# A new instruction order, engine choice and bank table for a two-layer transformer kernel on one core

## The chip, the core and the metric

The kernel runs on one core of a Trainium2 chip. The core has a matrix engine (TensorE, PE in the profile; its weight loads stand apart as PEld), a vector engine (VectorE, DVE), an engine for activation functions (ScalarE, ACT), a general engine (GpSimd, POOL) and a queue that issues the DMAs (SyncE, SP). Each takes its instructions in order from a queue of its own, and a semaphore makes one wait for another. The metric is device time in microseconds (us), lower is better.

## The reference

The input is one sequence of 2048 rows of 512 bf16 numbers. Four stages, each added to its input:

```python
x = x + A(layernorm(x))   # attention
x = x + B(layernorm(x))   # MLP
x = x + A(layernorm(x))   # the same weights again
x = x + B(layernorm(x))
# A: qkv = x @ wqkv; 32 heads of 16; causal, window of 256 keys;
#    softmax(q k^T / 4) v, then @ wo
# B: gelu(x @ w1 + b1) @ w2 + b2, hidden size 1792
```

## The kernel before, in words

All data stay on chip. The two layers make 32 tiles of 128 rows, handled as 16 *blocks* of two tiles (blocks 0 to 7 are the first layer, 8 to 15 the second). Each step has a name (`key`) that is used below:

- `lnq(b)` (L661): layer norm (`bs`, `ba` statistics on VectorE, `vp` and `pw` the inverse root, `xn` the scaling), a transpose to the layout that the matmul needs (`tx`, a DMA, L632; on TensorE, `tp`, for four tiles at the start and two at the end), and the Q projection (`q{b}_{i}`, steps of two matmuls) with its copy out of the accumulators (`qe`).
- `kv(b)` (L680): the K projection (`k`, copied out with a mask by `ke` on VectorE, L687) and the V projection (`v`, copied out by `ve`). Two DMAs a tile (`vs`, L702) make a second copy of V, moved by 64 rows.
- `attention(b)`: *score groups* `sc{b}_{g}` (L754; ten in a block, five in blocks 0 and 8), each followed by two exponentials on ScalarE (`ex{b}_{g}_0` and `_1`, L761) and one or two masks (`mk`, L782). The *value products* `pv{b}_0` and `pv{b}_1` (L804) take the masked exponentials of the first and the second half of the heads; in a full block one of them is 128 matmuls with their weight loads. Then follow `od` (L813), `rc` (L817), `nm` (L821), `ot` (L827), the output projection `op` and the addition `rs` (L849).
- `mlp(J)`: ten jobs of two or four tiles; the first matrix `m{J}_{fc}`, the bias and gelu on VectorE and ScalarE (`gb` L871, `ga` L874, `ge` L879), the second matrix `y{tau}`, the additions `xb` (L887) and `ya` (L894), and at the end the output DMA.
- `warm0` to `warm17` (L539): matmuls on zeros, put into the PE queue. Seven of them are 32 columns wide (`WSHORT`), the others 512.

These steps are 3098 nodes of a plan. What runs where and when is not computed but read from three tables: `_ORDER` is one list of all node numbers (each engine's queue is its own nodes in that order), `_ALT` lists the nodes that run on their second engine (a mask or `nm` on GpSimd in place of VectorE; `ve`, `qe` or `te` on ScalarE in place of VectorE; `vp` on VectorE in place of GpSimd), and `_BANKS` gives, in the order of use, the first of the eight accumulator banks that each group of matmuls takes. `_Plan.run` (L393) reads them, and asserts that no node stands before one that it depends on and that a bank is free:

```python
for i in _ALT:
    nodes[i]["eng"], nodes[i]["fn"] = nodes[i]["alts"][1]
for i in _ORDER:
    for g, k in nd["alloc"]:
        b = next(banks)
        gmap[g] = tuple(range(b, b + k))
```

`_Sched.op` (L62) then adds the waits: a step waits for whoever wrote what it reads, and for whoever last used what it overwrites, a bank among others. So a score group cannot start before an earlier exponential, copy or addition has emptied the banks that the table gives it.

Of the kernel before, what the change touches and what calls it, by code (L numbers as in the profile page):

```python
# [19 lines left out]
class _Sched:  # L20
# [147 lines left out]
    15, 34, 5, 0, 6, 14, 35, 7, 33, 28, 38, 29, 47, 8, 18, 23, 9, 36, 3, 26, 31, 10, 57, 37, 11, 22, 1, 40, 4, 24,  # L168
    2, 58, 59, 61, 17, 42, 62, 21, 60, 65, 41, 63, 19, 64, 68, 55, 32, 66, 107, 39, 69, 67, 20, 105, 50, 70, 3097,
    48, 30, 27, 53, 25, 106, 108, 71, 109, 49, 72, 110, 73, 16, 74, 114, 81, 75, 82, 111, 83, 84, 115, 85, 86, 116,  # L170
    112, 87, 88, 89, 113, 195, 153, 117, 127, 128, 151, 196, 129, 130, 154, 118, 152, 131, 119, 197, 155, 120, 156,
    98, 99, 100, 121, 12, 101, 90, 13, 102, 367, 91, 368, 104, 159, 92, 93, 157, 94, 103, 325, 76, 369, 199, 77,
    326, 95, 78, 200, 79, 370, 132, 80, 133, 96, 134, 135, 201, 323, 97, 203, 198, 137, 136, 158, 138, 205, 144,
    139, 202, 140, 145, 204, 141, 146, 160, 147, 122, 520, 217, 148, 123, 206, 124, 219, 143, 125, 208, 126, 46,
    218, 324, 43, 213, 209, 327, 328, 215, 166, 167, 168, 331, 169, 214, 207, 371, 176, 329, 177, 521, 373, 210,
    178, 330, 216, 179, 522, 171, 172, 180, 372, 161, 173, 211, 142, 174, 170, 56, 375, 220, 162, 376, 332, 163,
    164, 523, 175, 524, 221, 374, 377, 150, 212, 165, 149, 380, 378, 222, 188, 382, 189, 44, 190, 181, 45, 525,
    182, 381, 223, 385, 183, 224, 191, 386, 184, 384, 226, 225, 227, 54, 231, 232, 387, 379, 233, 526, 234, 383,
    333, 228, 185, 343, 388, 389, 334, 192, 229, 235, 344, 395, 194, 230, 335, 396, 345, 238, 346, 291, 390, 236,
    397, 239, 237, 347, 240, 336, 241, 348, 337, 349, 338, 242, 350, 244, 339, 243, 391, 399, 351, 401, 340, 341,  # L180
    352, 400, 245, 403, 342, 392, 402, 51, 353, 405, 52, 354, 355, 398, 356, 186, 360, 404, 357, 361, 362, 527,
    363, 393, 408, 364, 253, 409, 260, 261, 407, 254, 262, 410, 359, 413, 255, 246, 247, 415, 411, 256, 412, 257,
    248, 249, 250, 258, 414, 406, 564, 251, 273, 394, 274, 566, 263, 276, 416, 267, 268, 417, 565, 264, 270, 271,
    265, 277, 642, 285, 286, 423, 567, 418, 640, 275, 643, 528, 287, 529, 428, 272, 419, 282, 252, 283, 429, 288,
    259, 289, 641, 420, 308, 290, 309, 421, 424, 266, 310, 311, 279, 278, 644, 269, 422, 645, 284, 307, 280, 312,
    281, 313, 314, 315, 540, 425, 426, 568, 427, 541, 570, 316, 648, 542, 543, 649, 317, 569, 544, 318, 530, 531,
    319, 532, 187, 533, 572, 534, 193, 320, 574, 321, 646, 430, 431, 322, 647, 292, 573, 293, 294, 432, 577, 295,
    435, 579, 366, 576, 296, 545, 297, 436, 358, 571, 298, 433, 578, 546, 582, 434, 547, 437, 584, 548, 575, 550,
    438, 899, 551, 552, 650, 583, 553, 439, 651, 441, 652, 440, 653, 554, 900, 897, 585, 592, 654, 299, 549, 300,
    301, 593, 365, 302, 303, 304, 442, 581, 305, 594, 586, 535, 536, 898, 580, 596, 537, 306, 598, 538, 587, 901,  # L190
    539, 902, 597, 595, 600, 588, 557, 601, 660, 661, 662, 663, 599, 602, 605, 664, 558, 559, 607, 560, 655, 656,
    561, 457, 458, 606, 603, 610, 903, 657, 589, 658, 612, 904, 604, 453, 590, 459, 454, 476, 455, 477, 611, 485,
    486, 563, 609, 479, 591, 480, 482, 562, 613, 659, 470, 471, 483, 556, 905, 464, 465, 467, 478, 468, 484, 608,
    450, 460, 469, 461, 906, 451, 466, 446, 452, 447, 481, 443, 487, 448, 444, 473, 472, 462, 665, 474, 456, 614,
    666, 667, 445, 463, 615, 449, 475, 616, 684, 625, 626, 668, 617, 489, 686, 620, 618, 490, 491, 492, 685, 493,
    619, 621, 494, 669, 688, 687, 627, 690, 628, 622, 629, 495, 488, 623, 689, 496, 632, 692, 497, 694, 498, 624,
    691, 499, 500, 501, 630, 502, 693, 697, 504, 631, 505, 633, 1017, 506, 698, 507, 508, 634, 509, 1018, 510, 503,
    635, 699, 511, 702, 1019, 670, 512, 704, 700, 671, 672, 1020, 695, 673, 1021, 703, 674, 712, 696, 513, 514,
    701, 676, 714, 515, 706, 516, 517, 705, 518, 713, 519, 716, 638, 707, 717, 715, 718, 833, 720, 708, 721, 677,
    917, 1022, 918, 919, 709, 722, 920, 719, 710, 725, 921, 678, 727, 679, 680, 724, 681, 726, 730, 922, 636, 923,  # L200
    1023, 731, 912, 924, 728, 1024, 913, 723, 914, 915, 732, 729, 925, 711, 941, 637, 943, 734, 907, 908, 909, 733,
    910, 916, 926, 555, 735, 942, 639, 1025, 911, 736, 945, 934, 946, 935, 675, 737, 947, 738, 683, 949, 1026, 936,
    739, 948, 951, 937, 740, 938, 741, 742, 682, 950, 743, 944, 954, 744, 745, 955, 746, 747, 750, 952, 748, 940,
# [762 lines left out]
```

## Time and profile before

| what | value |
|---|---|
| time, median of 3 runs | 442.14 us (442.01 to 442.3) |
| profiled execution: span | 442.4 us, 0.26 us above that median; no other time of its own is shown |
| TensorE busy | 416.1 us (94%) |
| ScalarE busy | 386.4 us (87%) |
| VectorE busy | 341.0 us (77%) |
| GpSimd busy | 212.7 us (48%) |
| mean granted TensorE clock | 0.996 |

A matmul row's busy time reaches to its last result, and the next one starts before that, so 94% does not mean that 6% is all that could be saved. Idle time of an engine counts only where the chain of work that ended last runs through it.

### The profile page before, as it was taken

The numbers are of one execution on the slowest core, as the hardware profiler recorded it, in microseconds if no ns is written. First come the engines' busy times: TensorE is split into PE (matmuls) and PEld (weight loads), VectorE is DVE, ScalarE is ACT, GpSimd is POOL, SyncE is SP. The second block draws the span as 40 slices with busy tenths as digits, with TensorE's granted clock in tenths as the row PEclk, the third lists the DMA queues.
The fourth block names the chain that finished last, engine by engine and source line by source line (L and its number), as shares of the span: only waits on it lengthen the run. The fifth ranks groups of instructions, "written<-read, shape, count | busy, mean of one in ns | idle before, by whom it ended". The sixth has DMA issues, their size and how long they took to land.

```text
span 442.4 us, 16864 instructions
## 1 busy us (share of the span) xinstructions
PE 416.1 (94%) x7523; PEld 233.2 (53%) x7593; DVE 341.0 (77%) x638; ACT 386.4 (87%) x458; POOL 212.7 (48%) x236
## 2 busy tenths in 40 slices
PE   8997999988789997999999999999999999999997
PEld 4555657544444563554455455455555464444675
DVE  7997789788785599967698868877888576746762
ACT  4997999999889999889899989999897988999533
POOL 3566344363442674711575454634728165804411
PEclk9999999999899999999999999999999999999999
DMA  7686422004101012121031021100421014003002
GB/s 234 184 209 185 87 64 45 20 10 69 39 3 25 16 34 56 28 46 24 4 65 31 1 57 26 34 20 10 69 39 20 20 39 105 14 1 81 15 0 73
DMA packets 48116, 23.25 MB, mean 53 GB/s; under 512 B 33196, under 2 KB 48044, under 8 KB 48044
## 3 DMA queue, kind: packets, MB, share of 16 engines
q1 hardware_dynamic: 48044, 22.17, 22.2%
q8 instruction: 60, 0.98, 0.9%
q14 instruction: 12, 0.10, 0.1%
HBM read 8.00 MB, written 2.10 MB: 23 GB/s over the span
## 4 chain that ended last, share of the span: by engine, by line
PE 79%; ACT 11%; DVE 6%; issue 2%; DMA 1%; DVEq 0%
PE ps L653 59%; PE ps L754 9%; PE ps L804 9%; ACT E L761 9%; DVE OD L813 1%; PE ps L539 1%; DVE stat L599 1%; DVE X L849 1%; DMA xnTB<-xn 1%; ACT gT L879 1%; ACT L879 1%; DVE KT L687 1%; DVE E L782 0%; PE ps L639 0%; ACT QT L590 0%
## 5 line engine op out<-in xcount | busy, mean ns | idle before, releaser
L761 ACT ACTIVATE E<-ps 128x1024 bf16<-128x1024 f32 x300 | 284.2, 1033 | 28.7 <-PE ps L754 28.0
L782 POOL TENSOR_TENSOR E<-E,mask 128x512 bf16<-128x512 bf16 (+2 forms) x111 | 120.9, 1106 | 91.3 <-ACT E L761 91.0
L653 PE MATMUL ps<-W_sb,gT 128*128 128x512 bf16 (+1 forms) x434 | 112.2, 373 | 3.2 <-issue 2.2
L653 PE MATMUL ps<-xnTB,W_sb 128*128 128x512 bf16 (+1 forms) x541 | 107.8, 336 | 3.4 <-issue 1.8
L653 PEld LDWEIGHTS ps<-xnTB,W_sb 128*128 128x128 bf16 x560 | 52.0, 98 | 42.9 <-issue 4.1
L653 PE MATMUL ps<-xnTA,Wqkv_sb 128*128 128x256 bf16 x512 | 70.7, 273 | 0.9 <-ACT E L761 0.4
L782 DVE TENSOR_TENSOR E<-E,mask 128x512 bf16<-128x512 bf16 (+2 forms) x125 | 60.1, 500 | 13.3 <-ACT E L761 12.9
L754 PE MATMUL ps<-QT,KT 32*128 32x128 bf16 (+3 forms) x1920 | 60.3, 231 | 9.8 <-ACT E L761 5.6
L653 PEld LDWEIGHTS ps<-W_sb,gT 128*128 128x128 bf16 x462 | 41.2, 98 | 41.1 <-issue 3.6
L754 PEld LDWEIGHTS ps<-QT,KT 32*128 32x128 bf16 x1920 | 28.5, 92 | 59.1 <-ACT E L761 34.9
L653 PEld LDWEIGHTS ps<-xnTA,Wqkv_sb 128*128 128x128 bf16 x512 | 47.4, 98 | 20.2 <-issue 2.9
L813 DVE STREAM_TRANSPOSE OD<-ps 128x1024 f32<-128x1024 f32 x32 | 39.9, 1246 | 21.3 <-PE ps L804 20.7
L887 POOL TENSOR_TENSOR Xb<-X,b2all 128x512 f32<-128x512 bf16 x32 | 37.7, 1180 | 34.3 <-DVE X L894 33.9
L879 ACT ACTIVATE gT<-ps,b1T 128x512 bf16<-128x512 f32 (+1 forms) x80 | 42.6, 609 | 9.5 <-PE ps L653 9.4
L804 PE MATMUL ps<-E,Va 64*17 64x128 bf16 (+3 forms) x1920 | 44.3, 234 | 1.9 <-issue 0.8
L821 POOL TENSOR_TENSOR Nb<-OD,Rc 128x512 bf16<-128x512 f32 x25 | 26.4, 1058 | 38.7 <-DVE Rc L817 29.8
L804 PE MATMUL ps<-E,Vs 64*17 64x128 bf16 (+3 forms) x1920 | 44.9, 234 | 0.0
L599 DVE BATCH_NORM_STATS2 stat<-X 128x6 f32<-128x512 bf16 x64 | 42.9, 679 | 0.5
L804 PEld LDWEIGHTS ps<-E,Va 64*17 64x17 bf16 x1920 | 37.2, 85 | 11.6 <-issue 9.0
L871 DVE TENSOR_SCALAR gT<-ps,b1T 128x512 bf16<-128x512 f32 (+1 forms) x60 | 36.8, 632 | 6.6 <-PE ps L653 6.2
L687 DVE TENSOR_TENSOR KT<-ps,parmask 128x1024 bf16<-128x1024 f32 x32 | 38.7, 1211 | 3.6 <-PE ps L653 3.6
L804 PEld LDWEIGHTS ps<-E,Vs 64*17 64x17 bf16 x1920 | 38.0, 85 | 0.2
(55 smaller groups left out, 348.8 us busy)
## 6 DMA issues: line engine op xcount, KB each, us to landing
Vs<-Va SPq DMA_DIRECT2D x64, 68.0 KB, 2.0
W_sb<-in_B_w_dram SPq DMA_DIRECT2D x4, 512.0 KB, 4.8
out_dram<-X SPq DMA_DIRECT2D x15, 128.0 KB, 1.8
X<-in_A_x_dram SPq DMA_DIRECT2D x3, 512.0 KB
Wqkv_sb<-in_A_wqkv_dram SPq DMA_DIRECT2D x4, 256.0 KB, 4.5
W_sb<-in_B_w_dram SPq DMA_DIRECT2D x2, 384.0 KB, 7.1
W_sb<-in_B_w_dram SPq DMA_DIRECT2D x1, 768.0 KB, 5.0
Wqkv_sb<-in_A_wqkv_dram SPq DMA_DIRECT2D x1, 512.0 KB, 6.7
```

The source lines that it names most:

```text
L599: add("dve", lambda e, B, t=t, k6=k6: e.bn_stats(stat6[:, k6, :], X[:, t, :]), reads=["X%d" % t], writes=["st%d" % k6], key="bs%d" % (k + j))
L653: r = e.matmul(ps[:, B[g][0], cols], lhsT, rhs, start=st, stop=sp)
L687: add("dve", lambda e, B, g=g, i=i: e.tensor_tensor(out=KT[:, kb, 2 * i : 2 * i + 2].rearrange("p c m a q -> p a (c m) q"), in0=ps[:, B[g] ...
L754: x = e.matmul(ps[:, bk[r], o : o + n], KT[rows, kb, c, m].rearrange("p a q -> p (a q)"), QT[rows, c, q : q + n], start=True, stop=True)
L761: add("act", lambda e, B, g_=g_, gi=gi: e.activation(E[:, 2 * gi : 2 * gi + 2, e0 : e0 + 512], ps[:, B[g_][0] : B[g_][0] + 2, :], AF.Exp, ...
L782: fn = lambda e, B: e.tensor_tensor(out=Ew, in0=Ew, in1=Mw, op=ALU.mult)
L804: x = e.matmul(ps[32 * r : 32 * r + VW, B[g][par], c % 2 * 2 * P + lo : c % 2 * 2 * P + hi], V[rows, (2 * b + m // 2) % VR, c * HC + 2 * r ...
L813: add("dve", lambda e, B: e.transpose(OD[:, s].rearrange("p a c q -> p (a c q)"), ps[:, B[g][0] : B[g][0] + 2, :]), reads=["ps:" + g], wri ...
L821: return e.tensor_tensor(out=Nb[:, s, :].rearrange("p (k a d) -> p a k d", a=2, d=Dh), in0=sums[:, :, :, 0:Dh], in1=rc[:, :, :, None].to_b ...
L871: add("dve", lambda e, B, g=g, fc=fc: e.tensor_scalar(out=gT[:, fc, c0 : c0 + M], in0=ps[:, B[g][0], 0:M], scalar1=b1T[:, fc : fc + 1], sc ...
L879: add("act", lambda e, B, g=g, fc=fc: e.activation(gT[:, fc, c0 : c0 + M], ps[:, B[g][0], 0:M], AF.Gelu_apprx_tanh, bias=b1T[:, fc : fc + ...
L887: add("pool", lambda e, B, t=t, xs=xs: e.tensor_tensor(out=Xb[:, xs, :], in0=X[:, t, :], in1=b2all[:], op=ALU.add), reads=["X%d" % t, "b2a ...
```

## The change

Only the three tables change; every function, shape, loop and DMA stays, and the same 3098 nodes run. Cut to the lines that hold the nodes named below (973 is `sc4_6`, 977 `sc4_7`, 964 `pv4_0`) and the heads of the tables:

```diff
 _ORDER = [
-    15, 34, 5, 0, 6, 14, 35, 7, 33, 28, 38, 29, 47, 8, 18, 23, 9, 36, 3, 26, 31, 10, 57, 37, 11, 22, 1, 40, 4, 24,
...
-    969, 970, 756, 758, 757, 963, 971, 973, 962, 1027, 1028, 1041, 974, 1029, 759, 1030, 1031, 958, 977, 978, 964,
...
+    34, 15, 8, 0, 35, 14, 32, 19, 38, 21, 31, 36, 16, 5, 57, 37, 1, 22, 9, 40, 58, 2, 17, 4, 59, 61, 10, 28, 3, 42,
...
+    756, 977, 963, 757, 978, 962, 1041, 979, 964, 675, 940, 971, 980, 932, 973, 965, 787, 974, 682, 788, 865, 789,
...
 _ALT = [
-    67, 70, 75, 102, 109, 116, 121, 148, 165, 170, 185, 192, 198, 202, 211, 216, 337, 342, 370, 374, 378, 384, 389,
...
+    67, 70, 75, 102, 109, 113, 121, 165, 170, 185, 192, 198, 202, 207, 211, 337, 342, 370, 374, 379, 383, 384, 389,
...
 _BANKS = [
-    0, 1, 0, 1, 0, 2, 3, 2, 3, 5, 7, 0, 6, 5, 3, 2, 5, 4, 2, 4, 2, 3, 3, 5, 0, 1, 2, 6, 1, 5, 2, 4, 6, 1, 0, 2, 4, 6,
...
+    6, 7, 4, 6, 0, 1, 4, 2, 4, 2, 5, 7, 4, 3, 1, 2, 4, 6, 7, 0, 7, 1, 2, 6, 1, 5, 3, 1, 2, 4, 6, 2, 0, 2, 4, 1, 7, 6,
```

Counted with the plan's names: of TensorE's 1629 steps 1195 stand at another place in its queue, by 2 places in the median; 219 of the 658 groups of matmuls use another bank. 131 nodes change engine. Masks: 57 go from GpSimd to VectorE and 43 the other way, net 14 to VectorE (6 of 512 columns, 4 of 256, 4 of 768). Six `nm` and, net, four `vp` go to VectorE. Of the copies, net three (`ve`, `qe`) go from VectorE to ScalarE: `ve3`, `ve8`, `qe6_1`, `ve26` leave ScalarE; `ve11`, `ve19`, `ve21`, `ve25`, `qe14_0`, `qe14_1`, `qe15_0` come to it; `te2` and `te3` swap.

The stretches of the queues that are spoken of below, decoded (`x4` stands for four steps):

```text
start, PE    before: ... warm3 warm16 tp0 tp1 warm4 b1t warm14 warm11 warm9 q0_0x3 warm0 q0_0 k0_0x4 tp3 k0_1 tp2 k0_1x3 sc0_0
             after:  ... warm2 tp0 warm8 tp1 warm4 warm11 warm13 q0_0x3 k0_0 warm9 k0_0x3 q0_0 k0_1 tp2 tp3 k0_1x3 sc0_0
start, DVE   before: ib i5 i6 bs0 ... vp2 b1c xn3 xn2 ke0_0
             after:  ib bs0 ... vp2 i5 i6 xn2 xn3 ke0_0
34-45 us, PE before: sc1_5 q3_0 k3_0x2 pv1_0 q3_0 k3_1x2 q3_1 k3_1 q3_1 sc1_6 k3_1 q3_1x2 sc1_7 v6x4 v7x4 sc1_8 m0_2 ...
             after:  sc1_5 q3_0 k3_0x2 pv1_0 q3_1x2 sc1_6 q3_1x2 k3_1x4 sc1_7 v6x4 v7x2 sc1_8 v7x2 m0_4 ...
16-50 us, SP before: ... vs2_1 ldu2 ldwo tx6 vs2_0 ldb2 tx7 vs3_1 vs3_0 ldu0 ldu1 ldz3 vs5_1 tx32 tx33 ldz0 ldz1 vs4_0 tx8
             after:  ... ldu1 ldz0 vs3_1 ldz1 vs2_0 vs3_0 tx7 tx6 ldz2 vs2_1 ldz3 ldu0 vs5_0 vs4_1 tx32 tx33 vs4_0 ldu2 tx9 tx8 ldx12
105-123, PE  before: pv3_1 sc4_1 v13x2 sc4_2 v13x2 op6x4 sc4_3 op7x4 v12 sc4_4 v12x3 k7_0x4 sc4_5 sc4_6 q7_0x4 sc4_7 pv4_0
                     m2_5x4 m2_3 m2_4 sc4_8 m2_3x3 sc4_9
             after:  pv3_1 v13 sc4_1 q6_1x2 q6_0x3 q6_1 q6_0 v13 sc4_2 op6 v13 op6x3 op7 sc4_3 op7x3 sc4_4 v12x4 q7_0x2 sc4_5
                     q7_0x2 k7_0x4 sc4_7 pv4_0 sc4_6 m2_5x3 sc4_8 m2_5 m2_3x4 sc4_9
105-123, ACT before: ex4_1 (2) ex4_2 (2) ex4_3 (2) ex4_4 (2) ex4_5 (2) ex4_6_0 qe7_0 ex4_7_0 ex4_6_1 ex4_7_1 ex4_8 (2) ex4_9 (2)
             after:  ex4_1 (2) qe6_0 ex4_2 (2) ex4_3 (2) ex4_4 (2) ex4_5_0 qe7_0 ex4_7 (2) ex4_5_1 ex4_6 (2) ex4_8 (2) ex4_9 (2)
105-116, DVE before: od3_1 rc3_1 ot3_1 ve13 rs6 bs38 rs7 bs39 ba38 ba39 ve12 mk4_3_0 xn38 xn39 mk4_4_1 mk4_4_0 ke7_0 mk4_3_1
             after:  od3_1 rc3_1 xn14 qe6_1 ot3_1 ve13 rs6 bs38 rs7 bs39 ba38 ba39 vp38 ve12 mk4_2_1 xn39 mk4_3_1 mk4_3_0
                     mk4_1_0 xn38 mk4_4_1 mk4_4_0 ke7_0
```

In this region the bank table also names other releasers. `pv4_0` waits for the bank of `qe7_0` before, of `ex4_7_0` after; `sc4_7` for `ex4_6_0` before, `ex4_5_0` after; `sc4_8` for `ex4_7_1` and `od4_0` before, `ex4_6_0` and `od4_0` after.

On SP the loads `ldu` and `ldz` (pieces of the two MLP matrices) and `ldx12` (four input tiles) are issued in another order: `ldx12`, the tenth DMA before, comes after `tx8`, and `ldu2`, before ahead of `tx6`, after `tx33`.

360 rows, old and new, of tables (_ALT, _BANKS, _ORDER) are left out of this document.

## The prediction

> **What bounds the kernel now.** I read the page's head and its chain first, then the busy times by stage, the chain inside two stages, and the timeline of single rows.
>
> ```profile
> span 442.4 us, 16864 instructions
> PE 416.1 (94%) x7523; PEld 233.2 (53%) x7593; DVE 341.0 (77%) x638; ACT 386.4 (87%) x458; POOL 212.7 (48%) x236
> ...
> q8 instruction: 60, 0.98, 0.9%
> ...
> PE 79%; ACT 11%; DVE 6%; issue 2%; DMA 1%; DVEq 0%
> ```
>
> TensorE carries 79% of the chain that ended last, and its work is the same in both kernels. Only the other 21%, mostly ScalarE and VectorE, can be saved. The stages tell where that lies (columns: stretch, length, busy time of PE, PEld, DVE, ACT and POOL with their instructions, clock, DMA share, GB/s):
>
> ```profile
> 11.06:33.18 22.12, 20.57 (x357) 12.78 (x357) 21.12 (x39) 21.68 (x27) 12.56 (x17) 1.00 0.78 197
> 33.18:44.24 11.06, 8.84 (x212) 5.72 (x211) 8.60 (x15) 8.82 (x12) 7.65 (x8) 1.00 0.63 185
> 44.24:88.48 44.24, 43.13 (x800) 28.00 (x807) 37.50 (x72) 41.98 (x57) 18.97 (x21) 1.00 0.26 54
> 110.60:132.72 22.12, 18.17 (x427) 9.98 (x431) 17.23 (x33) 18.63 (x22) 9.66 (x13) 0.92 0.10 21
> 188.02:265.44 77.42, 74.96 (x1385) 39.70 (x1397) 60.00 (x118) 71.41 (x83) 34.73 (x37) 1.00 0.17 33
> 265.44:353.92 88.48, 86.62 (x1505) 45.18 (x1518) 70.77 (x121) 81.46 (x92) 43.98 (x47) 1.00 0.17 30
> ```
>
> From 11 to 33 us ScalarE is full (21.68 of 22.12). From 33 to 44 us nobody is full: PE and ACT both lose 2.2 us. From 110 to 133 us PE loses 3.95 us and ACT 3.49 us. From 44 to 88 us and after 188 us PE is busy 97 to 98% of the time: little is to be won there, but a late mask or copy would show. So what the change is worth is decided before 133 us.
>
> **The change part by part. The start.** The first score group waits for `ke0_0` (L687), and that for the last step of `k0_0`:
>
> ```profile
> 1.10 1.46 POOL L536 MEMSET Va<- 128x320 bf16 x1
> 1.36 1.38 DVE L521 TENSOR_SCALAR pidx<-pidx 128x2 int32<-128x2 int32 x1
> 2.77 0.17 DVE L523 TENSOR_SCALAR parmask<-pidx 128x2 f32<-128x2 int32 x1
> 8.29 0.73 DVE L627 TENSOR_SCALAR xn<-X,statmv,rstd 128x512 bf16<-128x512 bf16 x2 [0.76 <-POOL rstd L617]
> 9.40 1.22 DVE L687 TENSOR_TENSOR KT<-ps,parmask 128x1024 bf16<-128x1024 f32 x1 [0.38 <-PE ps L653]
> 11.13 1.94 ACT L761 ACTIVATE E<-ps 128x1024 bf16<-128x1024 f32 x2 [0.91 <-PE ps L754]
> ```
>
> The new order puts `k0_0` ahead of the last step of `q0_0` and a narrow warm-up in place of a wide one, so the 0.38 us wait can go; `xn` ends at 9.02, so no more can. Against it, `i5` (L521) and `i6` (L523) move from the start, where the wait for the input hides them, into the 0.76 us wait for `pw2`. L523 took 0.17 us; L521 took 1.38 us beside a GpSimd memset that ended at 2.56. If each takes 0.17 us, they are hidden; at 1.38 us the cover is gone and it costs 1.38 + 0.17 - 0.76 = 0.8 us. Ends: -0.4 and +0.4 us. ScalarE was idle 0.91 us before its first exponential, so the gain is passed on. I take **-0.2 us**, nearer to the L523 row, since only the short `pw2` runs beside it now.
>
> [...]
>
> **To 45 us.** Here the chain runs through VectorE's statistics for block 3 and a transpose (the first row from the chain, the second from SP's queue):
>
> ```profile
> 39.42 4.08 DMA xnTB<-xn
> ```
> ```profile
> 37.71 2.96 SPq L632 DMA_TRANSPOSE xnTB<-xn  x2
> ```
>
> `ve3` leaves ScalarE (0.6 us in the rows of L590 below) for VectorE (0.7 us), which is as full (21.12 of 22.12); VectorE in turn loses, ahead of `xn32`, two narrow masks and `xn8`. But MLP job 0 starts only when `tx33` has landed, at 43.50, 4.08 us after an issue that SP began late, because `tx32` held it from 37.71. Both stay behind `xn32` and `xn33`, with as many bytes of weights ahead of them as before (`ldu2` and `ldx12` now behind, `ldz0` and `ldz1` now ahead, 1 MB each way). So only what `xn32` gains is passed on: between -0.6 us (all that `ve3` frees) and +0.3 us (half a copy more on VectorE). I take **-0.3 us**. `ldu2`, issued behind `tx33`, lands some 4.8 us later by the row below, at about 46 us; its first reader, hidden job group 10 or above, stands some 20 steps of two matmuls (about 0.25 us) behind the start of job 0, at about 48 us. If that cover is gone, it costs the difference, up to 1 us. `ldx12` is read by block 6 only, so its move costs nothing.
>
> ```profile
> W_sb<-in_B_w_dram SPq DMA_DIRECT2D x4, 512.0 KB, 4.8
> ...
> L588 DVE CAST Va<-ps 128x512 bf16<-128x512 f32 x22 | 14.8, 676 | 3.4 <-PE ps L653 3.2
> L590 ACT ACTIVATE Va<-ps 128x512 bf16<-128x512 f32 x10 | 6.1, 625 | 1.1 <-PE ps L653 1.0
> ```
>
> **From 105 to 128 us**, the largest term:
>
> ```profile
> 103.33 1.72 PE ps L804 x118
> ...
> 107.25 0.42 PE ps L754 x12
> ...
> 107.70 8.46 ACT E L761 x9
> 116.16 0.50 ACT QT L590
> ...
> 116.79 2.32 PE ps L804 x125
> ```
> ```profile
> 113.00:116.40 3.40, 1.69 (x36) 1.01 (x28) 3.12 (x7) 3.40 (x5) 0.33 (x1) 1.00 0.19 39
> 116.50:119.90 3.40, 2.89 (x138) 2.16 (x132) 0.71 (x1) 3.00 (x4) 1.22 (x2) 0.50 0.20 41
> ```
> ```profile
> 106.67 0.09 PEld L754 LDWEIGHTS ps<-QT,KT 32*128 32x128 bf16 x1 [1.15 <-DVE OD L813]
> 105.53 1.94 ACT L761 ACTIVATE E<-ps 128x1024 bf16<-128x1024 f32 x2 [0.51 <-PE ps L754]
> 114.08 1.02 DVE L782 TENSOR_TENSOR E<-E,mask 128x768 bf16<-128x768 bf16 x2
> 114.38 0.40 PE L754 MATMUL ps<-QT,KT 32*128 32x256 bf16 x8 [1.25 <-ACT E L761]
> 121.30 3.77 ACT L761 ACTIVATE E<-ps 128x1024 bf16<-128x1024 f32 x4 [1.78 <-PE ps L754]
> ```
> ```profile
> L653 PE MATMUL ps<-xnTA,Wqkv_sb 128*128 128x256 bf16 x512 | 70.7, 273 | 0.9 <-ACT E L761 0.4 <-issue 0.3
> ```
>
> Three things are seen. First, `sc4_2` loaded a weight at 106.67, but its first matmul came at 107.25, 0.58 us later, though its semaphores were up. I read that as TensorE waiting for instructions: they come in 60 transfers of 16 KB, one for about 252 of its 15116 rows, and a value product eats a whole one; here they arrived 2.2 us after `pv3_1` ended (105.05). After the change nine steps of two matmuls (70.7 us for 512: 0.28 us a step, 2.5 us) and `sc4_1` (0.4 us) stand between the two, so this wait is covered. Worth: the 0.22 us that ScalarE lost before its next exponential (107.70 less 105.53 + 1.94).
>
> Second, `pv4_0` waited for nine exponentials and `qe7_0`. After the change its bank comes from `ex4_7_0`: counted from `ex4_1_0` that is 10 exponentials and two copies against 11 and one, so about 10.6 us of ScalarE against 11.1 us (105.53 to 116.66): -0.5 us. VectorE must have `mk4_4_0` by then; of the five instructions that it gets, `xn14` and `qe6_1` fall into its idle time behind `rc3_1`, and 0.9 us remain. Its masks were done at 115.1, and the product now starts at about 116.2: hidden, by 0.2 us.
>
> Third, `sc4_6` and `sc4_7` stood on exponentials (1.25 us for the first), yet ScalarE was then idle 1.78 us before block 4's last exponentials, since `pv4_0` and six MLP steps stood ahead of `sc4_8`. Now `sc4_6` stands behind `pv4_0` and three MLP steps ahead of `sc4_8`, with banks freed one exponential earlier, so ScalarE goes on almost without a gap: at most -1.8 us. In this time `pv4_0` ran at half clock, 2.32 us for 125 rows against 1.72 us for the 118 of `pv3_1`, after a stretch in which PE was busy 1.69 of 3.40 us. If the half clock comes again I get about -0.8 us for the whole region (`sc4_9` is then ready at about 122.2 against 122.9), without it -1.7 us. TensorE's idle time ahead of `pv4_0` remains some 2 us, so either can be; I take **-1.2 us**, the middle. The worse end is +0.7 us: masks late by all 0.9 us.
>
> [...] The trace has the length of the half-clock window (116.5 to 119.9 at 0.50) but not the cause: PE was half busy, its longest gap 1.25 us. [...]
>
> **Everything else.** By the mean durations below, VectorE gets 6 x 0.51 + 4 x 0.29 + 4 x 0.57 us of masks and 6 x 0.74 us of `nm`, and gives off 3 copies of 0.68 us: about +9 us, to 350 us, and GpSimd loses as many instructions. ScalarE gets 3 x 0.62 = 1.9 us, all after 188 us, where it has 6 to 7 us of slack in each of the two stages shown. The banks and the small shifts in TensorE's queue cost nothing where PE is full. I take **0**, and +-0.9 us as bounds: a third of PE's 4.3 us of idle time in those two stages, gained or doubled, scaled to the 310 us after 133 us.
>
> ```profile
> L782 DVE TENSOR_TENSOR E<-E,mask 128x512 bf16<-128x512 bf16 x59 | 29.6, 513 | 4.7 <-ACT E L761 4.6
> L782 DVE TENSOR_TENSOR E<-E,mask 128x768 bf16<-128x768 bf16 x47 | 26.0, 571 | 8.3 <-ACT E L761 8.2
> L782 DVE TENSOR_TENSOR E<-E,mask 128x256 bf16<-128x256 bf16 x19 | 5.4, 285 | 0.3 <-ACT E L761 0.2
> L821 DVE TENSOR_TENSOR Nb<-OD,Rc 128x512 bf16<-128x512 f32 x7 | 5.1, 736 | 0.2
> ```
>
> **Sum:** 442.4 - 0.2 - 0.3 - 1.2 + 0 = 440.7 us of span; the median stands 0.26 us below the span, so **440.4 us**.
>
> **The rivals.** (a) *More than that:* the clock stays full at 117 us (-1.7) and the start and the `ve3` term pay in full (-0.4 and -0.6): 439.7 us of span, 439.4 us. For it: PE's gaps there are spread otherwise. Against: a full VectorE to 33 us.
>
> (b) *Nothing arrives:* `tx33` lands where it did, since SP issues it behind `tx32` as before, so the first two terms are 0; the half clock comes again, and `pv4_0` waits for its masks, so the third is -0.3 us: 441.8 us. For it: the 4.08 us transfer ends a chain that ScalarE is not on. Against: `xn32` itself can come earlier.
>
> (c) *Slower, by VectorE:* the masks and `nm` that it takes over (10.9 us) stand in a strictly ordered queue ahead of value products and of the copies that free banks. If a third of them, 3.6 us, is exposed, the sum is 440.4 + 3.6 = 444.0 us; at 16% (1.7 us) the gain is gone, and from 24% on (2.6 us) it is slower. For it:
>
> ```profile
> 221.20:232.26 11.06, 10.74 (x183) 5.81 (x177) 10.87 (x22) 10.12 (x12) 7.73 (x9) 1.00 0.31 65
> ```
>
> In this stretch VectorE is full (10.87 of 11.06). Against: just there it gets nothing more; most of what it gets lies in 107 to 119, 277 to 293 and 375 to 391 us, and over the run it has 101 us idle.
>
> **How the numbers follow.** A change under 0.2% (0.9 us) cannot be told from none here. Chances: the forecast 0.37, (a) 0.15, (b) 0.18, (c) 0.30. (c) stands above (a) because its threshold, 16% of 10.9 us, is low against an engine that is full in several stretches. So faster 0.52, same 0.18, slower 0.30. The forecast's own range is 439.3 to 441.5 us: 0.9 us either way for everything else, and a little for the third term, whose -1.2 stands 0.5 us from -0.8 and -1.7. The range for all cases reaches from 438.5 us, (a) with 0.9 us off "everything else", to 444.0 us, (c) with a third exposed.
>
> **What would show it.** Right: the first exponential before 11.0 us; job 0's first matmul before 43.5 us; no weight load of `sc4_2` standing alone; ScalarE's 1.78 us gap near 120 us gone; the stage to 132.7 us shorter by 1 to 2 us, and PE's share after 188 us unchanged. Wrong: VectorE waited for in the rows of L804 and L754 by more than now, a second half-clock stretch, or job 0 waiting for `ldu2`.

## The result, and the profile after

The changed kernel takes 447.24 us (median of 4 runs, 446.5 to 447.77) beside 442.22 us for the kernel before: ratio 1.0112, 95% interval 1.0098 to 1.0127. It is 5 us slower. The forecast was 440.4 us, faster than before, with a range up to 444.0 us; the change went the other way, and the time lies outside the range.

First the head of the page and the chain of waits of the profile after:

```profile
span 444.9 us, 16862 instructions
PE 418.2 (94%) x7523; PEld 232.5 (52%) x7593; DVE 348.4 (78%) x659; ACT 389.3 (88%) x461; POOL 190.0 (43%) x212
...
PE 71%; DVE 10%; ACT 10%; DMA 4%; issue 3%; SPq 2%; POOL 0%; DVEq 0%
```

The engines' busy times moved about as counted: VectorE +7.4 us (+9 forecast), GpSimd -22.7, ScalarE +2.9 (+1.9 forecast). New is what the chain runs through: transfers and SP's queue hold 6% of it, against 1% before, and TensorE 71% against 79%.

The span grew by 2.5 us only, while the time grew by 5. The changed kernel's profiled execution took 446.92 us, 2.0 us more than its span, and in every later run the time stood 1.7 to 2.1 us above the span. The page of before, with a span of 442.4 us, therefore shows an execution of about 444.2 us: slower than any of the three times beside it, and with a half-clock window at 116.5 us. A later profile of the same kernel (run `b_self`, below) is the better reference:

```profile
span 440.0 us, 16864 instructions
PE 414.0 (94%) x7523; PEld 232.0 (53%) x7593; DVE 341.0 (78%) x638; ACT 386.5 (88%) x458; POOL 212.7 (48%) x236
```

Where TensorE waits shows in the table of its waits (what was waited for: us in total, times, the longest), first of `b_self`, then of after. L653 there is L645 here: the tables are 8 lines shorter.

```profile
PE ps L653 <- DMA xnTB<-xn: 0.6, 1, 0.6
```
```profile
PE ps L645 <- DMA xnTB<-xn: 2.4, 2, 1.6
PE ps L645 <- ACT E L753: 2.2, 7, 0.6
```

`xnTB` is the transposed input of the MLP. The longest of these waits is that of MLP job 3; this is the chain through it, after:

```profile
169.20 0.18 DVE rstd L603
169.38 0.07 issue
169.44 0.71 POOL rstd L609
...
170.18 0.43 DVE xn L619
...
170.67 2.17 SPq L624
...
172.94 2.44 DMA xnTB<-xn
175.38 0.05 issue
175.43 3.24 PE ps L645 x8
```

and these are SP's issue of the same two transposes and the job's first matmuls in `b_self`:

```profile
168.55 3.32 SPq L632 DMA_TRANSPOSE xnTB<-xn  x2
```
```profile
173.30 1.89 PE L653 MATMUL ps<-xnTB,W_sb 128*128 128x512 bf16 x8 [0.38 <-ACT E L761]
```

The input `xn43` was ready 2.1 us later than in `b_self` (170.59 against 168.52; 1.0 us of that is a lag that the trace of after already has at 162 us), the two transposes went out later, and job 3 waited for them, not for ScalarE. The wait had a second effect. These are the busy times in the stretch before 174.77 us and the next one, after (the 0.50 is the granted clock):

```profile
171.36:174.77 3.41, 1.55 (x35) 0.64 (x35) 3.37 (x7) 3.41 (x5) 2.37 (x3) 1.00 0.43 75
174.77:178.18 3.41, 2.75 (x7) 1.04 (x8) 1.29 (x3) 1.93 (x3) 1.05 (x1) 0.50 0.49 99
```

The job's eight matmuls then took 3.24 us in place of 1.89.

### The profile page after: what moved, and what is told of

Same layout as the page of the kernel before. It is cut to its first block, busy times and chain, and to the rows that moved or that the text cites. A ratio compares the mean times of both kernels' runs of the same rounds, so it can differ in the third digit from the quotient of the medians.

```text
span 444.9 us, 16862 instructions
## 1 busy us (share of the span) xinstructions
PE 418.2 (94%) x7523; PEld 232.5 (52%) x7593; DVE 348.4 (78%) x659; ACT 389.3 (88%) x461; POOL 190.0 (43%) x212
## 4 chain that ended last, share of the span: by engine, by line
PE 71%; DVE 10%; ACT 10%; DMA 4%; issue 3%; SPq 2%; POOL 0%; DVEq 0%
PE ps L645 54%; PE ps L746 8%; PE ps L796 8%; ACT E L753 7%; DMA xnTA<-xn 3%; SPq L624 2%; DVE Va L580 1%; DVE E L774 1%; DVE KT L679 1%; DMA xnTB<-xn 1%; PE ps L531 1%; DVE gT L863 1%; ACT gT L871 1%; DVE QT L580 1%; DVE xn L619 1%
## 5 line engine op out<-in xcount | busy, mean ns | idle before, releaser
L774 POOL TENSOR_TENSOR E<-E,mask 128x512 bf16<-128x512 bf16 (+2 forms) x97 | 103.8, 1084 | 114.7 <-ACT E L753 114.2
L645 PE MATMUL ps<-xnTB,W_sb 128*128 128x512 bf16 (+1 forms) x541 | 111.6, 338 | 5.4 <-DMA xnTB<-xn 2.4
L645 PE MATMUL ps<-W_sb,gT 128*128 128x512 bf16 (+1 forms) x436 | 109.0, 373 | 2.5 <-issue 2.1
L645 PE MATMUL ps<-xnTA,Wqkv_sb 128*128 128x256 bf16 x512 | 72.9, 274 | 2.4 <-ACT E L753 1.3
L645 PEld LDWEIGHTS ps<-xnTB,W_sb 128*128 128x128 bf16 x560 | 51.9, 98 | 43.3 <-issue 4.8
L774 DVE TENSOR_TENSOR E<-E,mask 128x512 bf16<-128x512 bf16 (+2 forms) x139 | 65.1, 493 | 10.1 <-ACT E L753 10.0
L645 PEld LDWEIGHTS ps<-W_sb,gT 128*128 128x128 bf16 x462 | 41.4, 98 | 43.2 <-issue 3.2
L645 PEld LDWEIGHTS ps<-xnTA,Wqkv_sb 128*128 128x128 bf16 x512 | 46.7, 98 | 24.9 <-issue 3.5
L871 ACT ACTIVATE gT<-ps,b1T 128x512 bf16<-128x512 f32 (+1 forms) x80 | 44.0, 607 | 8.3 <-PE ps L645 8.0
L796 PE MATMUL ps<-E,Va 64*17 64x128 bf16 (+3 forms) x1920 | 43.2, 230 | 2.9 <-ACT E L753 1.6
L796 PE MATMUL ps<-E,Vs 64*17 64x128 bf16 (+3 forms) x1920 | 43.9, 230 | 0.0
L813 POOL TENSOR_TENSOR Nb<-OD,Rc 128x512 bf16<-128x512 f32 x19 | 20.5, 1077 | 47.2 <-DVE Rc L809 43.4
```

The lines of the kernel that those rows point to most:

```text
L645: r = e.matmul(ps[:, B[g][0], cols], lhsT, rhs, start=st, stop=sp)
L774: fn = lambda e, B: e.tensor_tensor(out=Ew, in0=Ew, in1=Mw, op=ALU.mult)
L796: x = e.matmul(ps[32 * r : 32 * r + VW, B[g][par], c % 2 * 2 * P + lo : c % 2 * 2 * P + hi], V[rows, (2 * b + m // 2) % VR, c * HC + 2 * r ...
L813: return e.tensor_tensor(out=Nb[:, s, :].rearrange("p (k a d) -> p a k d", a=2, d=Dh), in0=sums[:, :, :, 0:Dh], in1=rc[:, :, :, None].to_b ...
L871: add("act", lambda e, B, g=g, fc=fc: e.activation(gT[:, fc, c0 : c0 + M], ps[:, B[g][0], 0:M], AF.Gelu_apprx_tanh, bias=b1T[:, fc : fc + ...
```

## The experiments

### Where the 5 us arise

The two orders hold the same set of nodes at position 1529 (about 220 us), and sets that differ by two at 1134 (about 160 us). So each stretch of the new tables can be put into the old ones: the order up to the cut from one table, the rest from the other, engines and banks with it.

```diff
-    for i in _ORDER:                      # all of it new
+    order = new[:1134] + [i for i in old if i not in new[:1134]]          # h_first
+    order = old[:1134] + (new up to 1529) + (old behind it)               # h_mid
+    order = old[:1529] + [i for i in new if i not in old[:1529]]          # h_late
```

> The kernel before once more, unchanged, for its spans and clocks. In the traces, 2.0 us lie between the span and the time of every execution of the changed kernel, while the profiled execution of before has a span of 442.4 us beside times of 442.0 to 442.3 us. Theory A (the profiled execution of before is a usual one): spans of about 442.4 us, so times of 444.4 us in this comparison, or another gap than 2.0 us. Theory B (it was an unusual one, with a half-clock window at 116.5 us that most executions do not have): times of 442.1 us, spans of 440.1 us, clock 1.000 in most executions, and no window at 0.50 before the end.

> The new tables up to about 160 us (the first 1134 nodes), the old ones behind. Theory 1 (the loss arises behind 160 us; the lag of TensorE's work between the two traces was -1.0 us there): 1.0 us faster than before, 441.2 us. Theory 2 (the gain of 1.0 us is only the half-clock window of before's profile, which before does not usually have): within 0.5 us of before, 441.8 to 442.6 us. Theory 3 (VectorE, loaded with more masks, costs from the start): 1 us or more slower, 443 us.

> The new tables for nodes 1134 to 1528 alone (about 160 to 220 us), the old ones elsewhere. Theory 1 (MLP job 3 waits 2.0 us for the transposes of its tiles, and the half-clock window that follows costs 1 to 1.5 us): 2 us slower than before, 444.1 us, with a window at 0.50 in those executions whose clock is below 1. Theory 2 (the transposes come late only because the part before them runs 1 us earlier): within 0.7 us of before. Theory 3 (VectorE): slower as well, but with the first matmul of job 3 waiting for a mask or a copy and not for the transpose.

> The new tables from node 1529 on (220 us to the end), the old ones before. Theory 1 (three single waits for transposes and value products, 0.43 us near 290, 0.78 us near 383 and 0.26 us near 410, as the lag between the traces shows): 1.4 us slower than before, 443.5 us. Theory 2 (these waits hang on the shift that the first half brings, by way of the places at which TensorE's instructions are fetched): within 0.5 us of before.

Measured against before, on one chip:

| run | median us | ratio to before, 95% interval |
|---|---|---|
| `b_self` (before once more) | 442.8 | 1.0005 (0.9992 to 1.0019) |
| `h_first` (new to 160 us) | 442.71 | 1.0001 (0.998 to 1.0023) |
| `h_mid` (new from 160 to 220 us) | 444.44 | 1.0040 (1.0025 to 1.0055) |
| `h_late` (new from 220 us) | 445.68 | 1.0068 (1.0052 to 1.0085) |

The last three add up to 1.0109, the whole change to 1.0112. By these times the new tables cost and gain nothing that can be measured up to 160 us (1 us either way), the next 60 us cost 1.8 us, and the rest 3.0 us. Theory B of `b_self` holds: its profiled execution has a span of 440.0 us, a time of 441.75 us and no half-clock window. Theory 2 of `h_first` holds.

That the three add up does not make them the account of the changed kernel. At the second cut both orders have done the same nodes; the last of them (`mk8_3_0`) ended at 217.50 us in `b_self` and at 220.84 us in after. Behind it stand 222.5 to 222.8 us in the seven traces that have the old tables there, 226.6 us in `h_late`, but only 224.0 us in after. So in its own trace the changed kernel loses 3.3 us up to the cut, a half-clock window among them, and 1.5 us behind it, where `h_late` loses 4.0: what the late tables cost depends on what runs ahead of them.

### The middle: VectorE, the transposes and the clock

In `h_mid`, `xn43` ends 1.75 us later than in `b_self` (0.6 us of that is a lag that this trace has already ahead of 160 us, under the old tables). In VectorE's queue the masks `mk6_1_0`, `mk6_3_0`, `mk6_3_1` (on GpSimd before), `xn18` and `bs20` now stand ahead of it; one mask, `mk6_4_1`, has gone to GpSimd. Job 3's first matmuls in `h_mid`:

```profile
174.55 1.90 PE L653 MATMUL ps<-xnTB,W_sb 128*128 128x512 bf16 x8 [1.10 <-DMA xnTB<-xn]
```

Two edits of `h_mid` were tried. The first gives the masks back:

```diff
 _ALT (with mask = on GpSimd)
+    mk6_1_0, mk6_3_0, mk6_3_1
```

> The kernel with the new tables for nodes 1134 to 1528 alone (1.8 us slower than before), with three of its masks (mk6_1_0, mk6_3_0, mk6_3_1) back from VectorE to GpSimd, nothing else. Theory V (VectorE: these masks, two other steps moved forward with them, make xn43 end 1.75 us later, so the transposes land later and job 3 waits): xn43 about 1.5 us earlier than without the edit, the wait of job 3's first matmul down by 1 us or more, the half-clock window gone from most executions, 442.4 to 443.0 us. Theory F (the transposes are late because an instruction fetch of TensorE falls on their issue): no change beyond 0.4 us, 444.0 to 444.8 us.

It came out no faster: 445.75 us, ratio 1.0060 (1.0041 to 1.008), by the ratios 0.9 us slower still, though the two intervals overlap. The wait for the transposes was gone, but the masks' way through GpSimd made `mk6_4_1` a microsecond later (169.66 against 168.63), and the value product `pv6_0` waited for that (its row names `vp42`, a step of VectorE that it does not need):

```profile
169.87 0.28 PE L805 MATMUL ps<-E,Va 64*17 64x256 bf16 x4 [1.78 <-DVE rstd L612]
175.51 1.59 PE L654 MATMUL ps<-xnTB,W_sb 128*128 128x512 bf16 x4 [0.20 <-DMA xnTB<-xn]
```

and `xn43` came later (171.28 against 170.26), for two reasons. Its root `pw42` stands on GpSimd behind those masks. And VectorE itself ran slower beside them: `vp42`, 0.17 us in `h_mid`, took 1.34 us and ended 0.02 us after `mk6_4_1` did, and `xn43` and `xn42`, 0.41 us each in `h_mid`, took 0.79 and 1.24 us. All six executions had a mean clock of 0.996; on the chip of this run 6 of 11 executions of before had that too, against 4 of 29 on the chip of `h_mid`. So moving the masks back cures nothing: neither engine has room for them there. That they alone made `xn43` late, as Theory V has it, is not shown by this run.

The second edit moves work in VectorE's queue only:

```diff
-DVE: bs43 ba43 rs10 ve17 bs42 ve15 ba42 vp42 bs20 xn43 xn42
+DVE: bs43 ba43 rs10 bs42 ba42 vp42 ve17 ve15 xn43 xn42 bs20
```

> The kernel with the new tables for nodes 1134 to 1528 alone, with four steps moved in VectorE's queue and nothing else: bs42, ba42 and vp42 ahead of the copies ve17 and ve15, and bs20 behind xn43 and xn42. Theory V (the chain of statistics behind xn43 is late in VectorE's full queue): xn43 ends about 0.5 us earlier, the wait of job 3's first matmul (1.26 us) falls by about as much, fewer executions have a half-clock window: 443.4 to 444.0 us beside 442.4 us for before (444.4 us without the edit). Theory F (instruction fetch on the issue of the transposes decides): the issue stays 1.6 to 2.2 us long and the time within 0.3 us of 444.4.

It took 443.26 us, ratio 1.0023 (1.0008 to 1.0039): by the two ratios 0.8 us of the 1.8 are gone, though the intervals overlap. Job 3's wait fell from 1.10 to 0.48 us, but its time went elsewhere: `ve15`, now later, frees a bank of `pv6_0` later. What differs is the clock. A mean clock of 0.995 to 0.996 was seen in 2 of 12 executions in place of 7 of 12, and the executions without it are alike: a median of 443.19 us here, 443.05 us in `h_mid`, about 0.7 us above the 442.4 us of such executions of before. So of the 1.8 us some 0.7 us are waits, and the rest comes from executions with a half-clock window.

```profile
170.32 0.28 PE L804 MATMUL ps<-E,Va 64*17 64x256 bf16 x4 [1.48 <-DVE Va L588]
...
175.36 1.47 PE L653 MATMUL ps<-xnTB,W_sb 128*128 128x512 bf16 x6 [0.48 <-DMA xnTB<-xn]
```

### The late part: SP's queue, VectorE and the fetch of instructions

In the trace of `h_late` TensorE has three waits that `b_self` doesn't have: 0.6 us at the K projection of block 13 (for the transposes `tx26`, `tx27`), 1.3 us at `pv12_0` (for the copies of V of tiles 24 and 25) and 1.3 us at MLP job 7 (for `tx58`, `tx59`); the expectations below count them up to 0.2 us longer. In the trace of after the second is not there, and the others are 0.25 and 0.75 us. SP's issues around the last two, in `h_late` (a group's length holds the waits inside it):

```profile
307.77 1.77 SPq L632 DMA_TRANSPOSE xnTB<-xn  x1
309.58 1.27 SPq L632 DMA_TRANSPOSE xnTA<-xn  x1
310.89 1.27 SPq L632 DMA_TRANSPOSE xnTB<-xn  x1
312.21 3.57 SPq L702 DMA_DIRECT2D Vs<-Va  x4
...
365.54 3.02 SPq L702 DMA_DIRECT2D Vs<-Va  x5
368.61 1.27 SPq L632 DMA_TRANSPOSE xnTB<-xn  x1
369.92 1.43 SPq L898 DMA_DIRECT2D out_dram<-X  x1
371.40 1.20 SPq L632 DMA_TRANSPOSE xnTB<-xn  x1
372.65 0.59 SPq L702 DMA_DIRECT2D Vs<-Va  x1
373.28 1.09 SPq L898 DMA_DIRECT2D out_dram<-X  x2
374.47 2.27 SPq L632 DMA_TRANSPOSE xnTB<-xn  x1
```

and in `b_self`:

```profile
303.02 0.46 SPq L702 DMA_DIRECT2D Vs<-Va  x1
306.49 1.55 SPq L632 DMA_TRANSPOSE xnTB<-xn  x1
308.09 1.23 SPq L702 DMA_DIRECT2D Vs<-Va  x2
...
369.53 2.51 SPq L632 DMA_TRANSPOSE xnTB<-xn  x2
```

The four copies stand behind `tx52`, which waits for `xn52` until 307.77 us, though the later of the two copies out of the accumulators that they read, `ve24`, had ended at 305.85 us. And `tx58` (at 374.47) stands at the end of an unbroken row of issues that began at 365.54 us, when the copy at its head got its data. Its input `xn58` was ready at 373.64 us, so the row cost it 0.8 us. Four edits of `h_late`:

```diff
 late_pool
+    mk14_0_0, mk14_1_0, mk14_2_0, mk14_2_1, vp58 on GpSimd
 late_shift
-    warm12, warm13, warm7, warm15: one matmul of 512 columns each
+    warm12, warm13, warm7, warm15: four matmuls of 32 columns each
 late_sp
-SP: tx52 tx29 tx53 vs24_0 vs25_1 vs24_1 vs25_0 ... out3 tx57 vs31_0 out1 out0 tx58 tx59
+SP: vs24_1 tx52 vs24_0 vs25_1 vs25_0 tx29 tx53 ... tx57 tx58 tx59 out3 vs31_0 out1 out0
 late_dve
-DVE: bs58 bs59 mk14_2_1 ba59 mk14_0_0 ba58 mk14_4_1 vp58 mk14_4_0 xn58 xn59
+DVE: bs58 bs59 ba59 ba58 vp58 mk14_2_1 mk14_0_0 xn58 mk14_4_1 mk14_4_0 xn59
```

> The kernel with the new tables from node 1529 on alone (3 us slower than before), with four masks of block 14 (mk14_0_0, mk14_1_0, mk14_2_0, mk14_2_1) and vp58 back from VectorE to GpSimd. Theory V: xn58 at least 1.5 us earlier, job 7's wait of 1.4 us for the transposes tx58 and tx59 gone, 444.3 us; the other two waits (k13, 0.8 us, and pv12, 1.4 us) stay. Theory F: the fetch at 375.1 us still lies on the issue of tx58 (2.27 us in place of 1.2) and job 7 still waits 1 us or more, 445.4 to 446.0 us.

> The kernel with the new tables from node 1529 on alone, with 12 more narrow matmuls in four of the warm-ups before any input is there, so that every later block of TensorE's instructions is fetched 24 instructions earlier; no other step, order or engine changes. Theory F: the fetch that fell 0.81 us behind the start of the issue of tx27 (2.37 us long) now falls some 0.95 us ahead of it, the issue takes 1.2 us, k13's wait of 0.8 us is gone, and the one at pv12 changes too since the fetch next to tx53 moves; tx58, where the fetch moves by 0.1 us only, stays as it is: 444.2 to 445.0 us. Theory V: the time depends on VectorE's queue, which is unchanged: 445.4 to 446.0 us.

> The kernel with the new tables from node 1529 on alone (3 us slower than before), with nine DMAs moved in SP's queue and nothing else: vs24_1 ahead of tx52 and the three other copies of tiles 24 and 25 right behind it (as before), and tx58, tx59 ahead of out3, vs31_0, out1, out0. Theory S (SP's queue is in order, so that these copies stood behind a transpose that waited for xn52 until 307.8 us, and tx58 behind ten DMAs that had all waited for ve31): the wait of pv12_0 (1.36 us) gone, that of job 7 (1.49 us) down to 0.5 us or less, 443.0 to 443.8 us. Theory V (VectorE's late xn58): only the first of the two, 444.2 to 444.8 us. Theory F: neither, 445.4 to 446 us.

> The kernel with the new tables from node 1529 on alone, with VectorE's steps ahead of xn58 in another order and nothing else: bs59, ba59, ba58, vp58 ahead of the masks mk14_2_1 and mk14_0_0, and xn58 ahead of mk14_4_1 and mk14_4_0. Theory V: xn58 ends 1.2 us earlier, job 7's wait for its transposes falls by about as much, 444.4 to 444.8 us. Theory S: tx58 cannot be issued before out0 is, at 374.4 us, so the wait stays above 0.8 us and the time within 0.5 us of 445.7.

| run | median us | ratio to before | wait at pv12_0, job 7 (us, by the rows of the traces) |
|---|---|---|---|
| `h_late` | 445.68 | 1.0068 (1.0052 to 1.0085) | 1.3, 1.3 |
| `late_pool` | 446.1 | 1.0071 (1.0049 to 1.0092) | 1.5, 0.2 |
| `late_dve` | 445.98 | 1.0082 (1.0068 to 1.0096) | 1.7, under 0.2 |
| `late_sp` | 444.28 | 1.0043 (1.0029 to 1.0058) | 0, 0.9 |
| `late_shift` | 455.38 | 1.0282 (1.0254 to 1.031) | 1.3, 1.6 |

`late_sp` gains 1.1 us by the two ratios, whose intervals just overlap; in the traces the part behind the cut is 224.6 us long in place of 226.6. The wait at `pv12_0` is gone (Theory S), that of job 7 only partly. `tx58` now went out at 372.15, but `tx59` behind it met a fetch of instructions that began at 373.41, and its issue took 2.48 us. `late_pool` and `late_dve` take job 7's wait away and gain nothing in time: `pv14_0` then waits 0.5 to 0.7 us for a mask. In `late_pool` that mask, `mk14_4_0` on VectorE, took 1.50 us beside a mask on GpSimd; in `h_late` it took 0.55. We read this as one shortage of VectorE and GpSimd at both ends, job 7's input and the masks. This is the row in `late_dve` (with a releaser that isn't the one; the last mask it needs, `mk14_4_0`, ends at 374.08):

```profile
374.13 0.28 PE L804 MATMUL ps<-E,Va 64*17 64x256 bf16 x4 [0.48 <-DMA xnTB<-xn]
```

`late_shift` was expected to gain 1 us and lost almost 10. The wait at block 13 did fall, from 0.6 us to under 0.2. But already ahead of 220 us, where the tables are the old ones, TensorE stood still for up to 2 us at a time, with no semaphore to wait for. That called for a test on both kernels.

### The blocks of instructions

```diff
 b_plus (of before), a_plus (of after)
-    four wide warm-ups: one matmul of 512 columns each
+    four wide warm-ups: four matmuls of 32 columns each    (24 instructions more)
 b_minus, a_minus
         for h in range(NWARM):
+            if h in WSHORT: continue                       (14 instructions fewer)
```

> [...] Theory W (the 10 us of the earlier shifted kernel came from the new tables behind 220 us or from the start): at most 1.5 us slower, 443.9 us.

> The changed kernel with the same 12 narrow matmuls in four of its warm-ups. [...] If its 5 us of loss come from a bad place of the blocks: faster or equal, 443 to 447 us. Theory W: 448.5 us.

> The kernel before without its seven narrow warm-ups (the rest unchanged), so that each block is reached 14 instructions later. [...] Theory W: within 0.5 us of before.

> The changed kernel without its seven narrow warm-ups. If its tables stand at a best place: 1 to 4 us slower than the changed kernel, 448 to 451 us. If the place of the blocks is what costs it 5 us: 2 us faster or more, 445 us or less. Theory W: within 0.5 us of 447.2.

| run | median us | ratio to before |
|---|---|---|
| `b_minus` | 442.5 | 0.9998 (0.9988 to 1.0008) |
| `b_plus` | 452.25 | 1.0223 (1.0203 to 1.0243) |
| after | 447.24 | 1.0112 (1.0098 to 1.0127) |
| `a_minus` | 449.95 | 1.0190 (1.0159 to 1.0221) |
| `a_plus` | 452.42 | 1.0224 (1.0206 to 1.0242) |

24 instructions at the start make the kernel before 9.7 us slower. At most 1.6 us of that lies ahead of the first exponential (12.28 us, 10.64 in `b_self`), where the full clock came later too (9.8 us, 4.6 in `b_self`, 7.26 in the old profile). Most of the rest is waits like this one, first in the chain of `b_plus`, then in the busy times of that stretch:

```profile
105.61 1.69 PE ps L805 x116
107.29 2.30 issue
109.59 0.25 PE ps L805
```
```profile
107.30:109.60 2.30, 0.01 (x1) 0.00 (x0) 0.00 (x0) 0.01 (x1) 0.00 (x0) 1.00 0.47 59
```

`pv3_1` stops before its last matmul for 2.30 us, and the whole core with it. In the record of the transfers a block of TensorE's instructions is fetched from 106.68 to 108.21 us; the matmul goes on 1.4 us after its end. Others like it are 0.9 us at 39.3 and 53.2 us, and 1.4 us at 184.1 us. Seven such waits, 7.1 us together, stand in this trace and none of them in `b_self`'s; no semaphore explains them, and each ended 1.2 to 1.5 us after a fetch had ended. We read them as waits for instructions, and Theory W of that run (at most 1.5 us slower) fails. That the old tables stand at the best place is not shown: 14 instructions fewer cost nothing (`b_minus`, ratio 0.9998).

The changed kernel is slowed by a shift either way, by the ratios 5.0 us (`a_plus`) and 3.5 us (`a_minus`, whose executions spread from 448.9 to 453.6 us), so neither of these places is better for it. Its own trace has at most one wait of this kind above 0.3 us (0.6 us, at 43.28 us), so the waits for instructions are not its 5 us. At +24 the two kernels are equally fast (1.0223 and 1.0224), but one point where two different losses meet doesn't say which order is better.

### Engines alone, and all edits together

```diff
 alt_old
     _ORDER, _BANKS of after
-    _ALT of after
+    _ALT of before
 after_fix
     after, with the edits of mid_dve, late_sp and late_dve
```

> The new order and banks throughout, but every step on the engine that it had before. Theory V: most of the 5 us is gone, 442.4 to 444 us, with xn43 and xn58 earlier. Theory F and the theory that the order alone decides: within 1 us of the changed kernel, 446.3 to 448.3 us. A GpSimd queue that now holds 14 more masks in an order made for fewer could add waits of its own; they would show as value products that wait for POOL.

> The changed kernel with all these edits together. If the waits for transposes and copies behind 160 us are what the change costs: the three waits (job 3, pv12, job 7) gone or halved, 2 to 3.5 us faster than the changed kernel, 443.5 to 445 us. If it is the fetch of instructions, or something that only the sum of the parts shows: within 1 us of the changed kernel, above 446 us.

`alt_old` took 464.79 us, ratio 1.0461 (1.0425 to 1.0496), by the ratios some 15 us more than the changed kernel. Both theories missed: the new order is made for the new engines. Its largest waits stand at value products, 2.9 us at `pv4_0` and 2.0 us at `pv12_0`.

`after_fix` took 446.68 us, ratio 1.0098 (1.0081 to 1.0116), 0.6 us better than the changed kernel, which is within the two intervals; 2 to 3.5 us were expected, and `mid_dve` and `late_sp` had gained 0.8 and 1.1 us by themselves. The named waits for transposes are gone, as its rows show, and these stand in their place: `pv6_0`, `sc9_4` (no semaphore; two fetches of instructions began at 222.1 and 225.9 us) and `pv14_0`.

```profile
170.85 0.28 PE L804 MATMUL ps<-E,Va 64*17 64x256 bf16 x4 [1.47 <-DVE Va L588]
...
224.82 0.18 PE L754 MATMUL ps<-QT,KT 32*128 32x64 bf16 x1 [0.59 <-issue]
...
374.95 0.28 PE L804 MATMUL ps<-E,Va 64*17 64x256 bf16 x4 [0.84 <-DVE E L782]
```

By the cut at 220 us its trace is 0.8 us ahead of that of after, and it loses 0.85 us against it behind the cut. So the named waits are not what the 5 us hang on: take one away and the next stands in its place. What remains between this kernel and before was not traced to single waits, and its cause stays open.

## Why the prediction was wrong

**The step that failed is "everything else: 0, +-0.9 us".** By the runs of the parts it was +4.8 us: 1.8 us from 160 to 220 us and 3.0 us behind. It was bounded by TensorE's idle time in two stages of the old profile, which bounds what can be gained there and says nothing of what can be lost; and a third of 4.3 us of idle time in 166 us, scaled to 310 us, is 2.7 us, not 0.9. The named cover was TensorE's full queue and ScalarE's slack. What lost its cover, as far as it was traced, was the way from VectorE's statistics over SP's queue and a transpose to the MLP, on which TensorE had been waiting 0.6 us and now waited 2.4 us; the clock made the wait of job 3 dearer (3.24 us for its eight matmuls at 0.50, 1.89 in `b_self`), and a part of the 5 us, perhaps half, is not traced to a single wait.

**Rival (c) had the engine, not the path.** VectorE's added masks did cost, but in stretches that the prediction had not named: three masks ahead of `xn43` near 165 us, four ahead of `xn58` near 370 us. The rival looked at value products and at banks; the loss came first through `xn` and its transpose, and moved to the value products when masks were given back or VectorE's steps reordered (`mid_pool`, `late_pool`, `mid_dve`, `late_dve`). Its upper value, 444.0 us with a third exposed, was 3 us short; it held no term for SP's queue, for the clock, or for transposes that meet a fetch.

**SP's queue was counted only up to 50 us.** The prediction went through SP's order at the start and in no later stage. `late_sp` shows what that left out in one stretch of `h_late`: 1.1 us by the ratios. In the changed kernel, whose trace has no wait at `pv12_0`, it is less.

**105 to 128 us, -1.2 us: most of its target was not there, and the stretch grew.** The half clock belonged to one unusual execution, and with it most of ScalarE's 1.78 us gap. In `b_self` the gap is 0.59 us; after, it is 0.39:

```profile
119.26 3.77 ACT L761 ACTIVATE E<-ps 128x1024 bf16<-128x1024 f32 x4 [0.59 <-PE ps L754]
```
```profile
118.24 5.61 ACT L753 ACTIVATE E<-ps 128x1024 bf16<-128x1024 f32 x6 [0.39 <-PE ps L746]
```

So the gap shrank by 0.2 us. But from the start of `ex4_1_0` to that of `ex4_9_1` eight traces with the old tables there take 17.3 us (`late_dve` 17.5, the old profile 18.5), and after, `h_first` and `after_fix` take 17.9 to 18.1: the term was +0.6 to +0.8 us. What the step had wrong is its first part. The nine Q and V steps that were to cover a wait of 0.58 us, worth 0.22, push `sc4_2` back, and the bank table now lets it wait for `ex4_1_1` in place of `ex4_1_0`. The next exponentials follow without a gap in `b_self` and not after, where the copy `qe6_0` and a wait for it stand between:

```profile
104.70 3.83 ACT L761 ACTIVATE E<-ps 128x1024 bf16<-128x1024 f32 x4 [0.50 <-PE ps L754]
```
```profile
104.84 1.94 ACT L753 ACTIVATE E<-ps 128x1024 bf16<-128x1024 f32 x2 [1.04 <-PE ps L746]
107.22 0.60 ACT L582 ACTIVATE QT<-ps 128x512 bf16<-128x512 f32 x1 [0.44 <-PE ps L645]
```

The times agree with that: `h_first` puts all terms up to 160 us together at 0.0 us, with an interval of 1.0 us either way, which excludes the sum of -1.7 us.

**The start, -0.2, and to 45 us, -0.3:** the first exponential came at 11.00 us and job 0 at 43.28 us after, against 11.13 and 43.58 in the old profile, which looks right; but in `b_self` they came at 10.64 and 42.59. Differences of this size are between executions, not kernels. The bet on `i5` and `i6` was right: in their new place they took 0.17 and 0.19 us and were done at 7.59 us, 0.5 us before `pw2` was. So `i6` did not wait for `pw2`, which ran beside it from 7.37 to 8.08 us.

**The sum's base was wrong.** "The median stands 0.26 us below the span" put two executions together. A time below the span of the profile should have been read as a sign that the profile is not of one of those executions.

**The clock.** The forecast took it as a matter of that one place. It is not tied to that place: inside the kernel it stood at 0.50 from 116.49 us in the old profile, from 174.77 us after, behind the new wait of job 3, and nowhere in `b_self`.

## What to carry to other kernels

An order that is made for one engine choice, and that a shift of the instruction blocks can slow by 2% (1.0223 in `b_plus`), can't be judged stage by stage from the old trace: list, for every stage, each transfer that TensorE reads with the time between its landing and its reader, and ask of each moved step whether it stands ahead of one of these in VectorE's, GpSimd's or SP's queue. Idle time bounds only a gain; for the loss, count these thin margins. Before any sum, compare the profile's span with the times, and look whether its clock has a window that other executions lack.

## What the runs showed of the hardware

**The half-clock windows of these traces lie on a grid.** In the 15 traces that have clock records, all eight windows at 0.50 inside the kernel began a whole number of steps of 3.413 us (30 to 96; 32 in the old profile, 49 after) after the clock first became full, and lasted one step. TensorE's busy share in the step ahead of them was 0.32 to 0.51 (0.50 in the old profile, 0.45 after); no step with a share of 0.55 or more was followed by one, and six with 0.46 to 0.52 were not. For the kernel before, 13 of 74 executions had a mean clock below 0.9975, with a median of 443.46 us against 442.37 us for the others: by these medians one window costs about 1.1 us. The executions come from four chips, and on one of them 6 of 11 had it. The clock first became full at 7.26 us in the old profile and at 4.6 us in `b_self`, two executions of one kernel, so the same wait can lie in another step of the grid: in the old profile the wait ahead of `sc4_6` lay in a step with a share of 0.50, and a window followed; in `b_self` a wait of 1.30 us lay in a step with 0.60, and none did. Half a step of work was not always enough to keep the clock.

**Instructions come in blocks, and a block can be late.** The pages of before and after list 60 transfers of 16 KB on the instruction queue (`q8`, 0.98 MB), one for about 252 of TensorE's 15,116 matmuls and weight loads. That they carry TensorE's instructions is our reading of the waits without a semaphore that end behind them. The longest of these was 2.30 us, in `b_plus`, and a shift by 24 instructions cost 2.2% of the time there.

**A transpose pays for such a fetch.** Behind 60 us the 18 traces hold 871 transposes, and 139 of them took more than 1.36 us to issue, up to 2.66. In 138 of these a fetch for TensorE began between 0.7 us ahead of the start of the issue and 1.2 us behind it. Of the 630 transposes without such a fetch all but one took 1.19 to 1.36 us.

**GpSimd slows some of VectorE's steps.** Behind 12 us in the 18 traces, VectorE's scalings `xn` and its masks of 512 columns never took more than 0.43 us while GpSimd stood still. With GpSimd busy for more than half of their time they took up to 1.83 and 1.87 us, and about four in ten took over half as long again. The statistics `bs` and the copies `ve` (0.7 us) took the same either way. So a mask that moves from one engine to the other also changes what its neighbours take, and the prediction's sum of mean durations has no such term.
